# One tile per batch for the gated MLP's columns, and output weights read in two layouts

## The chip, the cores and the metric

The kernel runs on one core of one Trainium2 chip. The metric is device time of one execution in microseconds. All matrix work is in float32 or in pairs of rounded float32 parts ("high" and "low"), since the result is compared in float32.

## What is computed

Three layers follow one another: attention of 4,096 rows and 256 state rows to each other, a gated MLP, and a soft mixture of experts whose routing runs over all 4,608 rows.

```python
scores = scale * np.matmul(x, state.transpose(0, 1, 3, 2))
a = softmax(scores);           xread = np.matmul(a, state)
a2 = softmax(scale * np.matmul(state, x.transpose(0, 1, 3, 2)))
sread = np.matmul(a2, x)
x = concatenate([xread, sread])                # 4608 rows of 512
xn = x / sqrt(mean(x * x) + 1e-06) * rms_g
h = silu(xn @ w_gate) * (xn @ w_val)           # 512 -> 1536
x = h @ w_out                                  # 1536 -> 512
logits = x @ phi                               # 512 -> 32 slots
d = softmax(logits, over rows)
slot_input = d.T @ x                           # 8 experts x 4 slots
slot_out = relu(slot_input @ w1[e]) @ w2[e]    # 512 -> 1024 -> 512
out = softmax(logits, over slots) @ slot_out
```

The kernel never forms `h @ w_out` for all rows. It takes the logits from `h` through the folded matrix `wphi` = w_out phi, sums `E^T h` over the rows (E: exponentials of the logits) and multiplies by w_out once at the end.

## The kernel before

**Tiling.** The rows are eight batches of 512, g = 0 to 7, and a group of 256 with the state's rows (`sread`, group 8). The 1,536 MLP columns are three chunks c of 512, each of four tiles of 128. The work proceeds in units (g, c, t): one tile of 128 columns for 512 rows. A unit has a gate half and a value half (gv 0 and 1): `main_mm` issues six products 128x512 of `A` (normalised attention, high and low part) with the batch's weights `wp`; ScalarE makes `sg` = silu (L476), VectorE makes `hT` = value times `sg` (L485) and later turns it in 32x32 squares in place (`turn`, L492). Four products a chunk add to the logits (`lg_mm`). `sw` makes `wp` for one chunk and half (eight products on TensorE, a ScalarE copy L443, a VectorE step L444).

**A batch's end.** When its third chunk is done, `post1` to `post3` update the running maximum and make E. Then `slot_h` multiplies E with the batch's turned `hT`: for each chunk, each 32-row block and each of four squares of rows one product of 32x32 weights with 128 columns, into four PSUM banks (two from the pool `mm`, which the units use too, two from `misc`); four VectorE steps (L599) add them to `acc`. All products of float32 take two instructions.

**Order.** A stage is what runs while one batch's units run: stage 0 has batch 0 and the first chunk of batch 1 (16 units), stage 1 the other 8 of batch 1, each later stage 12. A table `at(unit, place, step)` fixes at which unit, and at which of two places in it, a step of the preparation for later batches is put; the queues then run in that order. The slot products of batch g stand at about the third unit of stage g+1. DMAs go out on SyncE's queue, in order.

**Weights.** They lie in memory as the bits of float64. `wload` fetches 1 MB, `wconv` makes float32 of it: two ScalarE operations (L179, L182), six of VectorE (two each of L195, L199, L203) and two adds on GpSimd (L207). The order is gate and value weights, then six loads of w_out. A converted w_out is stored as float32 (`w_out32`, six times 512 KB), read back for the end, and transposed on TensorE and multiplied with phi in `wphi_part` (six parts in stages 0 and 1). `conv1` at the table's units does the next conversion and load.

**Buffers.** `k8` holds 19 tiles of 8 KB a partition, for raw weights, `A`, `hT` and, later, the experts' weights, which `prefetch` asks for.

**The end.** After the sread group come the product with w_out, the experts in pairs, whose weights stream in, and the output.

```python
for c in range(NC):
    h = HT.pop((g, c))[:, : gsize(g), :]...
    for b in range(nb):
        o = 32 * (b % 4)
        for f in range(4):
            fs = slice(32 * f, 32 * f + 32)
            mm(pss[f][o : o + 32, c * P : (c + 1) * P], ET[fs, b, :], h[fs, :, b, :], ...)
```

## Time and profile before

| | before |
|---|---|
| median of 3 runs (lowest to highest) | 778.26 us (777.56 to 781.26) |
| the profiled execution | 776.07 us |
| its span | 774.0 us |
| TensorE (PE) busy | 666.7 us, 86% |
| weight loads (PEld) busy | 421.1 us, 54% |
| VectorE (DVE) busy | 464.0 us, 60% |
| ScalarE (ACT) busy | 335.1 us, 43% |
| GpSimd (POOL) busy | 107.5 us, 14% |
| read from HBM, written | 73.47 MB, 12.06 MB |

A busy share is a mean over the span. The chain of waits tells which engine sets the end; the rows below are from it, from the groups of instructions by cost, and from views of single stretches. PE is TensorE's products, PEld its weight loads, which overlap them. PEclk is the granted share of TensorE's full clock. The line numbers in the rows are those of the kernel before; nearly all products are recorded at the helper's line L85, transposes at L107, so the tiles tell them apart.

### The profile page before, as it was taken

To read this page: it belongs to the slowest core of one execution; us is meant where nothing else is said; L and a number is where in the kernel's file an instruction comes from. 1 tells how busy PE (TensorE), PEld (TensorE's weight loads), DVE (VectorE), ACT (ScalarE), POOL (GpSimd) and SP (SyncE) were. 2 spreads that over 40 slices of the span, in tenths; PEclk is the share of its full clock that TensorE was granted. 3 is DMA by queue.
4 is the path that set the end of the run, shared out by engine and by line. 5 is a ranking of instruction groups with operands and counts; after the bars stand their busy time and mean duration, and the time that the engine had idled before them with its cause. 6 is when DMAs were issued, how large, how long until landed. Compare 5 with 4: busy or idle time off the path is not lost.

```text
span 774.0 us, 17621 instructions
## 1 busy us (share of the span) xinstructions
PE 666.7 (86%) x7660; PEld 421.1 (54%) x7660; DVE 464.0 (60%) x942; ACT 335.1 (43%) x519; POOL 107.5 (14%) x129
## 2 busy tenths in 40 slices
PE   6496789997996999799799989989996996969990
PEld 4153456455554665455555656655654685944350
DVE  6848798875783477446546754675693475342251
ACT  6247473564382447236443833654321452200061
POOL 2304364220011011000101010110100000001340
PEclk9669898999999999999899999999997997988995
DMA  9920054511101011001101010100028033886948
GB/s 352 409 82 5 0 218 166 189 61 82 42 19 61 4 55 34 27 6 55 61 1 49 10 58 3 55 3 1 1 101 310 28 109 113 322 273 242 386 149 338
DMA packets 31972, 86.65 MB, mean 112 GB/s; under 512 B 1816, under 2 KB 3992, under 8 KB 29080
## 3 DMA queue, kind: packets, MB, share of 16 engines
q1 hardware_dynamic: 31608, 85.47, 30.2%
q8 instruction: 60, 0.98, 0.5%
q14 instruction: 16, 0.13, 0.1%
q10 hardware_dynamic: 288, 0.07, 0.0%
HBM read 73.47 MB, written 12.06 MB: 110 GB/s over the span
## 4 chain that ended last, share of the span: by engine, by line
PE 68%; DVE 18%; issue 7%; ACT 3%; DMA 1%; POOL 0%; DVEq 0%; ACTq 0%; POOLq 0%
PE mm L85 41%; PE misc L85 17%; PE lg L85 4%; PE misc L107 4%; DVE wp L444 2%; DVE hT L492 2%; DVE w L195 2%; PE so L85 2%; DVE w L203 2%; DVE hT L485 2%; DVE w L199 1%; ACT wp L443 1%; DMA raw_t<-in_w_gate_dram 1%; DVE wo L195 1%; DVE rinv L423 1%
## 5 line engine op out<-in xcount | busy, mean ns | idle before, releaser
L85 PE MATMUL mm<-A,wp 128*128 128x512 f32 x1152 | 302.9, 411 | 0.3 <-DVE hT L485 0.3
L85 PEld LDWEIGHTS mm<-A,wp 128*128 128x128 f32 x1152 | 216.0, 194 | 95.6 <-issue 44.1
L485 DVE TENSOR_TENSOR hT<-mm,sg 128x512 f32<-128x512 f32 x102 | 69.5, 683 | 73.9 <-PE mm L85 48.1
L476 ACT ACTIVATE sg<-mm 128x512 f32<-128x512 f32 x102 | 61.1, 599 | 97.3 <-PE mm L85 84.5
L85 PE MATMUL misc<-w,stTg 64*32 64x512 f32 x768 | 77.9, 624 | 15.8 <-DVE wp L444 7.9
L492 DVE STREAM_TRANSPOSE hT<-hT 128x512 f32<-128x512 f32 x102 | 69.6, 694 | 22.6 <-PE lg L85 22.6
L85 PE MATMUL mm<-hT,E 32*32 32x128 f32 x1632 | 54.0, 307 | 30.8 <-issue 26.1
L443 ACT CAST wp<-misc 128x512 fp32r<-128x512 f32 x96 | 51.5, 589 | 48.0 <-PE misc L85 47.6
L476 ACT ACT_TABLE_LOAD x27 | 34.6, 1283 | 78.6 <-PE mm L85 78.2
L444 DVE TENSOR_TENSOR wp<-misc,wp 128x512 fp32r<-128x512 f32 x96 | 61.6, 674 | 6.1 <-ACT wp L443 5.3
L85 PE MATMUL misc<-hT,E 32*32 32x128 f32 x1632 | 53.9, 308 | 12.4 <-issue 11.4
L85 PEld LDWEIGHTS mm<-hT,E 32*32 32x32 f32 x1632 | 38.5, 109 | 39.8 <-issue 30.5
L85 PEld LDWEIGHTS misc<-w,stTg 64*32 64x32 f32 x768 | 14.7, 107 | 61.5 <-issue 25.7
L85 PEld LDWEIGHTS misc<-hT,E 32*32 32x32 f32 x1632 | 37.6, 109 | 15.1 <-issue 12.8
L599 DVE SCALAR_TENSOR_TENSOR acc<-acc,al,mm 128x384 f32<-128x384 f32 x16 | 9.1, 610 | 52.3 <-PE misc L85 52.3
L85 PE MATMUL lg<-hT,wphi 128*32 128x512 f32 (+1 forms) x216 | 38.4, 580 | 0.3 <-DVE hT L485 0.3
L85 PE MATMUL mm<-xsg,wh 128*128 128x256 f32 x192 | 36.0, 289 | 0.0
L207 POOL TENSOR_TENSOR w<-w,raw 128x512 int32<-128x512 int32 x20 | 29.5, 1485 | 39.7 <-ACT wp L443 16.1
L302 POOL TENSOR_TENSOR a<-a,asum 128x1024 f32<-128x1024 f32 x7 | 13.6, 1947 | 142.9 <-PE mm L85 65.8
L415 POOL TENSOR_TENSOR rinv<-ra,rs_magic 128x128 int32<-128x128 int32 x10 | 4.1, 413 | 207.7 <-DVE ra L411 207.7
L85 PEld LDWEIGHTS mm<-xsg,wh 128*128 128x128 f32 x192 | 30.6, 196 | 2.5 <-issue 1.6
L396 ACT CAST A<-aT 128x1024 fp32r<-128x1024 f32 x8 | 8.4, 1046 | 46.7 <-DVE aT L392 37.0
(187 smaller groups left out, 895.5 us busy)
## 6 DMA issues: line engine op xcount, KB each, us to landing
ew<-in_w_dram SPq DMA_DIRECT2D x27, 1024.0 KB, 7.7
xT<-in_x_t_dram SPq DMA_DIRECT2D x8, 1024.0 KB, 5.0
xn<-in_x_n_dram SPq DMA_DIRECT2D x8, 1024.0 KB, 4.9
raw<-in_w_val_dram SPq DMA_DIRECT2D x6, 1024.0 KB, 17.0
out_dram<-ob SPq DMA_DIRECT2D x6, 1024.0 KB, 12.0
ew_w<-in_w_dram SPq DMA_DIRECT2D x5, 1024.0 KB, 9.8
raw<-in_w_gate_dram SPq DMA_DIRECT2D x4, 1024.0 KB, 14.2
raw_t<-in_w_out_dram SPq DMA_DIRECT2D x3, 1024.0 KB, 5.8
```

Of the source, the lines that this page charges most:

```text
L85: nc.tensor.matmul(out=o, lhsT=lhsT, rhs=rhs, start=start, stop=stop)
L107: nc.tensor.transpose(o, i, ident)
L195: nc.vector.tensor_scalar(out=dst[:, h], in0=dst[:, h], scalar1=EXP_LO, scalar2=EXP_HI, op0=ALU.max, op1=ALU.min,)
L203: nc.vector.scalar_tensor_tensor(out=a[:, h], in0=hi[:, h], scalar=-0x40000000, in1=a[:, h], op0=ALU.bitwise_and, op1=ALU.bitwise_or,)
L207: nc.gpsimd.tensor_tensor(out=a[:, h], in0=a[:, h], in1=rnd[:, h], op=ALU.add)
L302: (eng or nc.gpsimd).tensor_tensor(out=a3, in0=a3, in1=asum.unsqueeze(2).to_broadcast([P, 32, 32]), op=ALU.mult)
L443: nc.scalar.copy(t[:, r, 0, :], ps)
L444: nc.vector.tensor_tensor(out=t[:, r, 1, :], in0=ps, in1=t[:, r, 0, :].bitcast(F32), op=ALU.subtract)
L476: nc.scalar.activation(out=sg, in_=ps, func=AF.Silu)
L485: nc.vector.tensor_tensor(out=HT[g, c][:, q // (2 if g == sread_group else 1), :], in0=ps, in1=sg, op=ALU.mult)
L492: nc.vector.transpose(out=h, in_=h)
L599: nc.vector.scalar_tensor_tensor(out=o, in0=o, scalar=Q[g, "al"], in1=i, op0=ALU.mult, op1=ALU.add)
```

## The change

1. `hT` of a batch is one tile of 24 KB a partition (`k24`, two buffers, paid for by six of the 19 `k8` buffers), and `slot_h` takes all twelve column tiles in one product: 64 products of 384 columns a batch in place of 192 of 128. The sread group, which keeps two tiles, has products of 256 and of 128 columns.
2. w_out is also given to the kernel transposed, as float64 bits like the others (`w_out_t`, six more loads of 1 MB). `wphi_part` multiplies the converted transposed tile with phi directly: the transposes on TensorE and the copies on ScalarE go. The six loads and conversions of w_out itself, now for `w_out32` alone, go one to each of the stages 1 to 6.
3. The low part of `A` is made on GpSimd for all batches, before for batches 2 to 7 only.
4. At the start one conversion stands behind the first batch's normalisation (`att_ss`, `att_A`) in place of ahead of it.
5. In the stages, `sw` of the two halves of a chunk stands in two units following one another, before at one place.
6. Some raw weights and expert weights lie in thirds of `k24` tiles (`IN_HT`, `more_slices`), and the last stage asks for three loads at its unit 4 where it asked for two at unit 0 and two at unit 8.

The diff's core:

```diff
-        return big.tile([P, 4, 512], dt, tag="k8", bufs=19, name=f"{name}_{cnt[name]}")
+        return big.tile([P, 4, 512], dt, tag="k8", bufs=13, name=f"{name}_{cnt[name]}")
+    def k24(name, dt=F32):
+        return big.tile([P, 12, 512], dt, tag="k24", bufs=2, name=name)
...
-    order += [(3, c) for c in range(NC)]
+    order += [(gv, c) for gv in (2, 3) for c in range(NC)]
...
-        (nc.gpsimd if b > 1 else nc.vector).tensor_tensor(
+        nc.gpsimd.tensor_tensor(
             out=A[:, :, 1, :], in0=aT, in1=A[:, :, 0, :].bitcast(F32), op=ALU.subtract
...
-        for c in range(NC):
-            h = HT.pop((g, c))[:, : gsize(g), :].rearrange("p a b -> p (a b)").rearrange(
-                "p (q b j) -> p q b j", q=4, j=32
-            )
+        if g == sread_group:
+            parts = [(0, 8, HT.pop((g, 0))), (8, 4, HT.pop((g, 1))[:, :2, :])]
+        else:
+            parts = [(0, NF, HT.pop(g))]
+        for q0, q, h in parts:
+            h = h.rearrange("p a b -> p (a b)").rearrange("p (q b j) -> p q b j", q=q, j=32)
             for b in range(nb):
...
-                        pss[f][o : o + 32, c * P : (c + 1) * P], ET[fs, b, :], h[fs, :, b, :],
+                        pss[f][o : o + 32, 32 * q0 : 32 * (q0 + q)], ET[fs, b, :], h[fs, :, b, :],
...
     def wphi_part(c, j):
-        wo = WO.pop((c, j))
-        wt = k4("woT", [4, 2 * P])
-        for i in range(2):
-            ps = misc()
-            for d2 in range(2):
-                for k in range(2):
-                    o = (2 * d2 + k) * P
-                    q = 2 * i + d2
-                    transpose(ps[:, o : o + P], wo[:, k, q * P : (q + 1) * P])
-            nc.scalar.copy(wt[:, 2 * i : 2 * i + 2, :].rearrange("p a f -> p (a f)"), ps)
+        wt = WOT.pop((c, j))
+        ps = misc()
+        for k in range(2):
+            mm(ps[32 * k : 32 * k + 32, :], phis[:, 2 * j + k, :], wt[:, k, :])
+        if j == 0:
+            WPP[c] = k2("wpp")
+            nc.vector.tensor_copy(WPP[c][:64], ps[:64])
+            return
+        wp = WPP.pop(c)
+        nc.vector.tensor_tensor(out=wp[:64], in0=ps[:64], in1=wp[:64], op=ALU.add)
         ps = misc()
         for q in range(4):
-            mm(ps[32 * q : 32 * q + 32, : 2 * P], phis[:, q, :], wt[:, q, :])
-        wp = k2("wpp")
-        nc.vector.tensor_copy(wp[:, : 2 * P], ps[:, : 2 * P])
-        ps = misc()
-        for k in range(2):
-            mm(ps[:, 32 * k : 32 * k + 32], wp[:, k * P : (k + 1) * P], r32)
+            mm(ps[:, 32 * q : 32 * q + 32], wp[:64, q * P : (q + 1) * P], r32[:64])
...
-        conv1()
         att_ss(0)
         att_A(0)
+        conv1()
         sw(0, 0, 1)
...
                     at(4 * i - o, 2, sw, nb, c, 0)
-                    at(4 * i - o, 2, sw, nb, c, 1)
+                    at(4 * i - o + 1, 2, sw, nb, c, 1)
+            if g < 7:
+                at(4 if g == 1 else 1, 1, wload, 1)
+                at(6 if g == 1 else 2, 2, wconv, 1)
...
-                at(0, 2, prefetch, 2)
-                at(8, 1, prefetch, 2)
+                at(4, 2, more_slices)
+                at(4, 2, prefetch, 3)
```

Three places show how the instructions move. The first is TensorE at the end of batch 2's slot products, in stage 3; `mm<-A` are main products, `misc<-w,stTg` is `sw`, `lg` the logits. Before, 96 rows of slot products stand here, the last two of which are shown:

```order
L85 MATMUL mm<-hT_2578,E 32x128 x2
L85 MATMUL misc<-hT_2578,E 32x128 x2
L85 MATMUL mm<-A_2568,wp_2599 128x512 x6
L85 MATMUL mm<-A_2568,wp_2731 128x512 x6
L85 MATMUL mm<-A_2568,wp_2746 128x512 x6
L85 MATMUL lg<-hT_2725,wphi 32x512 x4
L85 MATMUL misc<-w_700,stTg 32x512 x8
L85 MATMUL misc<-w_780,stTg 32x512 x8
L107 MATMUL misc<-ident,sT 128x128 x4
```

And now, where 32 rows of slot products end:

```order
L88 MATMUL mm<-hT,E 32x384 x2
L88 MATMUL misc<-hT,E 32x384 x2
L88 MATMUL mm<-A_2225,wp_2294 128x512 x6
L88 MATMUL mm<-A_2225,wp_2387 128x512 x6
L88 MATMUL mm<-A_2225,wp_2452 128x512 x6
L88 MATMUL lg<-hT,wphi 32x512 x4
L88 MATMUL misc<-w_695,stTg 32x512 x8
L110 MATMUL misc<-ident,sT 128x128 x4
```

The products have three times the columns and stand before the same main products; the second `sw` has left this unit.

The second place is VectorE in the same stretch; `E` is the exponentials' turn, `c_all` and `cs` belong to the softmax over slots. Before:

```order
L566 STREAM_TRANSPOSE E<-E 128x512
L301 RECIPROCAL asum<-asum 128x32
L570 TENSOR_REDUCE cmax<-c_all 128x4
L571 TENSOR_TENSOR c_all<-c_all,cmax 128x128
L485 TENSOR_TENSOR hT_2725<-mm,sg 128x512
L611 TENSOR_REDUCE cs<-c_all 128x4
L612 TENSOR_SCALAR cs<-cs 128x4
L615 RECIPROCAL cs<-cs 128x4
L616 TENSOR_TENSOR c_all<-c_all,cs 128x128
L599 SCALAR_TENSOR_TENSOR acc<-acc,al,mm 128x12x32 x2
L599 SCALAR_TENSOR_TENSOR acc<-acc,al,misc 128x12x32 x2
L485 TENSOR_TENSOR hT_2725<-mm,sg 128x512
```

And now:

```order
L589 TENSOR_REDUCE cmax<-c_all 128x4
L497 TENSOR_TENSOR hT<-mm,sg 128x512
L590 TENSOR_TENSOR c_all<-c_all,cmax 128x128
L206 TENSOR_SCALAR wo_2500<-wo_2500 128x512 x2
L210 TENSOR_SCALAR wo_2500<-wo_2500 128x512 x2
L214 SCALAR_TENSOR_TENSOR wo_2500<-raw_2415,wo_2500 128x512 x2
L632 TENSOR_REDUCE cs<-c_all 128x4
L633 TENSOR_SCALAR cs<-cs 128x4
L636 RECIPROCAL cs<-cs 128x4
L637 TENSOR_TENSOR c_all<-c_all,cs 128x128
L620 SCALAR_TENSOR_TENSOR acc<-acc,al,mm 128x12x32 x2
L620 SCALAR_TENSOR_TENSOR acc<-acc,al,misc 128x12x32 x2
```

The six operations of a w_out conversion have come between the maximum over slots (`cmax`) and the steps of `acc`.

The third is VectorE at the start; L408 begins the chain that makes `rinv`, the rows' norms, and L435 ends it. Before, with more operations of the same conversion ahead:

```order
L195 TENSOR_SCALAR w_218<-w_218 128x512
L199 TENSOR_SCALAR w_218<-w_218 128x512
L203 SCALAR_TENSOR_TENSOR w_218<-raw_104,w_218 128x512
L408 TENSOR_SCALAR rv<-misc 128x128
L411 TENSOR_SCALAR ra<-rv 128x128
```

And now:

```order
L432 SCALAR_TENSOR_TENSOR ra<-ra,rv 128x128
L435 SCALAR_TENSOR_TENSOR rinv<-ra,rinv 128x128
L404 TENSOR_TENSOR aT<-aT,misc 128x1024
L206 TENSOR_SCALAR w_216<-w_216 128x512
L210 TENSOR_SCALAR w_216<-w_216 128x512
L214 SCALAR_TENSOR_TENSOR w_216<-hT,w_216 128x512
```

The conversion follows the end of the chain and `aT`, where it stood ahead of the chain's start; A's low part has left VectorE.

## Rows read from the trace of the kernel before

**Rows 1.** Page, part 4: the chain, share of the span by engine.
```profile
PE 68%; DVE 18%; issue 7%; ACT 3%; DMA 1%; POOL 0%; DVEq 0%; ACTq 0%; POOLq 0%
```

**Rows 2.** Page, part 5: group | busy us, mean ns | idle before it us, releaser.
```profile
L85 PE MATMUL mm<-hT,E 32*32 32x128 f32 x1632 | 54.0, 307 | 30.8 <-issue 26.1
...
L85 PE MATMUL misc<-hT,E 32*32 32x128 f32 x1632 | 53.9, 308 | 12.4 <-issue 11.4
```

**Rows 3.** Windows, nine slots: length, PE, PEld, DVE, ACT, POOL busy, PEclk, DMA, GB/s.
```profile
584.30:596.54 12.24, 8.02 (x385) 6.36 (x385) 0.78 (x4) 0.00 (x0) 0.00 (x0) 0.64 0.87 316
644.40:657.10 12.70, 7.41 (x384) 5.90 (x384) 4.31 (x10) 2.88 (x6) 0.00 (x0) 0.68 0.29 97
685.10:692.00 6.90, 3.21 (x192) 2.52 (x192) 0.56 (x3) 0.00 (x0) 0.00 (x0) 0.84 0.98 348
sum 92.29, PE 53.76 PEld 43.51 DVE 19.25 ACT 17.21 POOL 11.69; mean PE 5.97 PEld 4.83 DVE 2.14 ACT 1.91 POOL 1.30
```

**Rows 4.** Chain of waits, batch 2's slot stretch: start us, length us, what.
```profile
306.94 1.15 issue
...
309.99 3.48 issue
...
313.91 5.91 PE mm L85 x18
```

**Rows 5.** Windows view, batch 2's slot products ahead of the first gap.
```profile
303.40:306.94 3.54, 3.54 (x246) 3.08 (x246) 3.40 (x7) 2.19 (x3) 2.32 (x2) 1.00 0.02 7
```

**Rows 6.** Page, parts 1 (busy, instructions) and 3 (queue: packets, MB, share).
```profile
PE 666.7 (86%) x7660; PEld 421.1 (54%) x7660; DVE 464.0 (60%) x942; ACT 335.1 (43%) x519; POOL 107.5 (14%) x129
...
q8 instruction: 60, 0.98, 0.5%
```

**Rows 7.** Windows view, 18 main products behind the slots of batches 1, 3, 4.
```profile
243.85:249.25 5.40, 5.40 (x23) 4.09 (x26) 2.82 (x5) 1.27 (x1) 0.00 (x0) 0.79 0.00 0
385.23:391.54 6.31, 6.31 (x23) 4.79 (x26) 2.87 (x5) 1.28 (x1) 0.00 (x0) 0.66 0.00 0
454.14:458.45 4.31, 4.31 (x23) 3.30 (x26) 2.78 (x5) 1.27 (x1) 0.00 (x0) 1.00 0.02 4
```

**Rows 8.** Timeline of TensorE, a logits group: start us, length us, what.
```profile
319.74 1.06 PE L85 MATMUL lg<-hT,wphi 128*32 128x512 f32 x8
```

**Rows 9.** Timeline of TensorE, one part of wphi.
```profile
122.98 1.16 PE L107 MATMUL misc<-ident,wo 128*128 128x128 f32 x8
...
130.90 0.64 PE L85 MATMUL misc<-woT,phis 128*32 128x256 f32 x8
132.08 0.63 PE L85 MATMUL misc<-r,wpp 128*128 128x32 f32 x4 [0.54 <-DVE wpp L639]
```

**Rows 10.** Timeline of VectorE, then of TensorE, at the start.
```profile
28.70 0.42 DVE L195 TENSOR_SCALAR w<-w 128x512 f32<-128x512 f32 x1
...
33.67 0.28 DVE L408 TENSOR_SCALAR rv<-misc 128x128 f32<-128x128 f32 x1
...
38.93 2.05 PE L85 MATMUL misc<-rinv,ident 128*128 128x128 f32 x8 [8.92 <-DVE rinv L423]
```

**Rows 11.** Page, part 5: making of the per-batch weights on TensorE.
```profile
L85 PE MATMUL misc<-w,stTg 64*32 64x512 f32 x768 | 77.9, 624 | 15.8 <-DVE wp L444 7.9
```

**Rows 12.** Timeline of VectorE, behind batch 2's slot products.
```profile
313.93 1.14 DVE L599 SCALAR_TENSOR_TENSOR acc<-acc,al,mm 128x384 f32<-128x384 f32 x2 [6.80 <-PE misc L85]
```

**Rows 13.** Timeline of VectorE, one conversion of w_out.
```profile
132.02 2.41 DVE L195 TENSOR_SCALAR wo<-wo 128x512 f32<-128x512 f32 x2
...
134.48 0.75 DVE L199 TENSOR_SCALAR wo<-wo 128x512 int32<-128x512 int32 x2
135.15 1.28 DVE L203 SCALAR_TENSOR_TENSOR wo<-raw,wo 128x512 int32<-128x512 int32 x2
```

**Rows 14.** Page, part 6: DMA issues, count, KB each, median us to landing.
```profile
ew<-in_w_dram SPq DMA_DIRECT2D x27, 1024.0 KB, 7.7
...
raw<-in_w_val_dram SPq DMA_DIRECT2D x6, 1024.0 KB, 17.0
```

More of the change, by code (lines that the diff above doesn't have):

```diff
@@ L133 @@
     w_out32 = dram.tile([DFF, DM], F32, name="w_out32")
-    bits = {0: w_gate.bitcast(I32), 1: w_val.bitcast(I32), 3: w_out.bitcast(I32)}
+    bits = {
+        0: w_gate.bitcast(I32), 1: w_val.bitcast(I32), 2: w_out_t.bitcast(I32),
+        3: w_out.bitcast(I32),
+    }
     order = [(0, 0), (1, 0), (0, 1), (1, 1), (0, 2), (1, 2)]
-    order += [(3, c) for c in range(NC)]
+    order += [(gv, c) for gv in (2, 3) for c in range(NC)]
     to_load = [(gv, c, j) for gv, c in order for j in range(2)]
@@ L139 @@
     to_conv = list(to_load)
-    RAW, W, WO = {}, {}, {}
+    RAW, W, WOT = {}, {}, {}
     def wload(n):
@@ L146, in wload @@
             gv, c, j = to_load.pop()
-            n_raw = 18 - len(to_load)
-            if n_raw in IN_TMP:
+            n_raw = 24 - len(to_load)
+            if n_raw in IN_HT:
+                i = IN_HT[n_raw]
+                t = HT[1][:, 4 * i : 4 * i + 4, :].bitcast(I32)
+            elif n_raw in IN_TMP:
                 t = tmp.tile([P, 4, 512], I32, tag="raw", name=f"raw_t{n_raw}")
@@ L163 @@
     begun = []
+    IN_HT = {2: 0, 3: 1, 4: 2, 11: 1, 12: 2}
+    HT = {1: k24("hT")}
     IN_TMP = (1, 9, 13, 15, 17)
@@ L209, in wconv @@
                 )
+            if gv == 2:
+                WOT[c, j] = d2
             if gv == 3:
-                WO[c, j] = d2
                 r0 = c * 512 + 2 * j * P
@@ L447, in sw @@
         WP[b, c, gv] = t
-    HT, LGP = {}, {}
+    LGP = {}
     xsg_t = {}
@@ L479, in main_h, with hT_rows, hT_chunk @@
     def main_h(g, c, q, ps, sg):
-        if q == 0:
-            if g == sread_group and c == 1:
-                HT[g, 1] = HT[g, 0][:, 2:, :]
-            else:
-                HT[g, c] = k8("hT")
-        nc.vector.tensor_tensor(
-            out=HT[g, c][:, q // (2 if g == sread_group else 1), :], in0=ps, in1=sg, op=ALU.mult
-        )
+        if g == sread_group:
+            if q == 0 and c != 1:
+                HT[g, c // 2] = k8("hT")
+        elif g not in HT:
+            HT[g] = k24("hT")
+        nc.vector.tensor_tensor(out=hT_rows(g, c, q), in0=ps, in1=sg, op=ALU.mult)
+    def hT_rows(g, c, q):
+        return hT_chunk(g, c)[:, q // 2 if g == sread_group else q, :]
+    def hT_chunk(g, c):
+        if g == sread_group:
+            return HT[g, c // 2][:, 2 * (c % 2) : 2 * (c % 2) + 2, :]
+        return HT[g][:, 4 * c : 4 * c + 4, :]
     def turn(g, c, q):
-        h = HT[g, c][:, q, :]
+        h = hT_rows(g, c, q)
         nc.vector.transpose(out=h, in_=h)
@@ L498, in lg_mm @@
         lg = LGP[(g,)]
-        hT = HT[g, c][:, :n, :].rearrange("p a b -> p (a b)").rearrange("p (q t) -> p q t", q=4)
+        hT = hT_chunk(g, c).rearrange("p a b -> p (a b)").rearrange("p (q t) -> p q t", q=4)
         for q in range(4):
@@ L675, in sread_prep, with more_slices @@
         xsg_t["xsg"] = xsg
-    WH = {}
+    WH, slices = {}, []
+    def more_slices():
+        x = k24("x")
+        slices.extend(x[:, 4 * i : 4 * i + 4, :] for i in range(3))
     def w_split(gv, c):
@@ L710, in prefetch @@
                 return
-            k = loads.pop()
-            if home is None:
+            k, at_home = loads.pop(), home
+            if home is None and slices:
+                t = at_home = slices.pop(0)
+            elif home is None:
                 t = k8("ew")
+            elif home not in exp_pool:
+                t = home
             else:
@@ L722, in prefetch @@
             nc.sync.dma_start(out=t, in_=src)
-            EW[k], ew_home[k] = t, home
+            EW[k], ew_home[k] = t, at_home
     def take(k):
@@ L735, in conv1 @@
         wconv(n)
-        if to_load and (to_load[-1][0] < 2 or len(RAW) < 3):
+        if len(to_load) > 6 and (to_load[-1][0] < 2 or len(RAW) < 3):
             wload(n)
@@ L967 @@
                     lg_mm(*now)
-                    for q in range(gsize(now[0])):
-                        at(u + q // 2, 2 - q // 2, turn, *now, q)
+                    for q in range(0, 4, 2 if now[0] == gs else 1):
+                        at(u + q // 3, 2 - q // 3, turn, *now, q)
                     if now[1] == NC - 1:
@@ L976 @@
                         at(u + 2, 1, slot_h, pg)
+                        if pg == gs - 1:
+                            at(u + 2, 1, more_slices)
             if u == len(halves) - 1 and t == 0:
@@ L993 @@
     keep_warm(6)
-    for q in range(gsize(gs)):
+    for q in (0, 2):
         turn(gs, NC - 1, q)
```

10 lines of the change are left out of this document (4 added, 6 removed).

## The prediction, made before the changed kernel ran

> **What bounds the kernel now.** I read the chain of waits first. It runs through TensorE for 68% of the span, and 7% of it is "issue", time in which an engine waited for nothing that the profile shows [rows 1]. So the question is what TensorE does, and where it stands still for no visible reason. The list of costliest groups answers the second part: the products of `slot_h`, the ones that read `hT` and `E`, carry 26.1 and 11.4 us of idle time released by "issue", 37.5 us together [rows 2]. That is most of the chain's 7%, 54 us of 774.
>
> Next I cut the span into the nine stretches from the first slot product to the next main product. They last 92.29 us, in which TensorE is busy 53.76 us [rows 3]. The chain inside batch 2's stretch shows where the rest is: two gaps, 1.15 and 3.48 us, with nothing else waited for, and after them 18 main products that take 5.91 us [rows 4]. After batch 4's stretch the same 18 take 4.31 us at a granted clock of 1.00; after batch 3's they take 6.31 us at 0.66, after batch 1's 5.40 us at 0.79 [rows 7]. So a long gap is paid twice: TensorE stands still, and then the next products run partly at the lower of its two clocks, 1.2 instead of 2.4 GHz.
>
> What is the gap? Ahead of the first gap of batch 2 lie 246 products and 246 weight loads in 3.54 us [rows 5]; 136 ns for two, where the main products take 4.31 us for 18, 240 ns for one [rows 7]. The queue that carries instructions moved 0.98 MB in 60 packets, and TensorE has 7,660 products and 7,660 loads, so a packet holds about 256 of them [rows 6]. I read the gaps as TensorE using up its code faster than it is brought. A slot stretch has 384 products and 384 loads, three packets' worth, in under 6 us of work.
>
> **The change part by part.** The forecast is summed against the profiled execution, 776.07 us (span 774.0 and 2.1 us around it).
>
> *Slot products.* 192 products of 128 columns per batch (two instructions each) become 64 of 384. Instructions go from 768 to 256 a batch, columns stay. What is left of the time? The logits give the price of a column in this type: 8 instructions on 4 column strips, so two rounds of 512 columns, take 1.06 us [rows 8], 133 ns for 128 columns. A slot batch runs on 16 squares of 32x32, so 24 rounds; active time is 5.85 us a batch, from the 53.76 us less the two slow batches and the short one, 35.1 / 6 [rows 3], hence 244 ns a round, of which 111 ns are not columns. After the change there are 8 rounds of 398 + 111 ns: 4.1 us. Bounds: 3.2 us if the 111 ns vanish, 5.85 us if nothing shrinks. I take 4.1, because the columns are measured and the loads stay one per round.
> The two slow batches, 8.02 and 7.41 us of busy time at a clock of 0.64 and 0.68 [rows 3], shrink by the same 4.1 / 5.85, to 5.6 and 5.2; the short group has 4 rounds of 256 and 4 of 128 columns, with the same 111 ns: 2.5 us. New total 6 x 4.1 + 5.6 + 5.2 + 2.5 = 37.9 against 92.3: **-54.4 us**, of which 37.5 are the gaps. With 256 products and loads in 4.1 us a packet lasts as long as two did before, so I forecast no gap.
>
> The Trainium skill (Runtime: NRT & Kernel Launch, section on instruction fetch mechanics) says that code comes in 16 KiB blocks of 256 instructions and that crossing a block is mostly hidden. The block agrees with the 0.98 MB in 60 packets [rows 6]; "mostly hidden" does not agree with 37.5 us of gaps [rows 2]. By that rule the gaps would be something else and would stay; this is rival 3.
>
> *Main products behind a gap.* Batches 1, 2 and 3 lose 1.1, 1.6 and 2.0 us there against batch 4 [rows 4, 7]; without gaps the clock has no reason to fall: **-4.7 us** (0 if it falls anyway).
>
> *`wphi`.* Per part, 16 transposes, 8 products and 4 small ones take 1.16 + 0.64 + 0.63 us of TensorE, with 0.54 us of waiting [rows 9]; six parts: 14.6 us. Now a part is two products of 512 columns on two strips, two rounds, 1.06 us by the logits row; and every second part has eight small instructions, twice 0.63. Sum 6.4 + 3.8 = 10.2: **-4.4 us** (bounds 0 and -4.4; the waiting stays). ScalarE's copies go too; they were not on the path.
>
> *The start.* The conversion that stood ahead of the normalisation on VectorE, from 28.70 to 33.67 us, goes behind it; TensorE waited 8.92 us for that chain [rows 10]. At best everything after moves up 5 us; but the second half of the value weights is then converted later, and the first unit wants it. I take **-2 us** (0 to -5).
>
> *Weights per batch.* The two makings of a chunk's weights go to neighbouring units. TensorE waited 7.9 us in all for VectorE between them [rows 11]; I take **-5** (0 to -7.9).
>
> *The six moved conversions.* One w_out conversion per stage 1 to 6 now stands on VectorE right behind the slot's exponent, ahead of the four `acc` steps and the next `hT`. One costs VectorE 0.75 + 0.75 + 1.3 us undisturbed, and 2.41 for the first two instead of 0.75 where another engine disturbs it: 2.8 to 4.5 us [rows 13]. Before, VectorE idled 6.80 us in this place, waiting for TensorE's slot products [rows 12]. That cover shrinks to about 4 us. After the slot TensorE has two half units (2 x 6 x 0.24 = 2.9 us) before it wants the banks that `acc` frees, and a third before the logits want the next `hT`. VectorE: conversion 4.5 from the slot's start, row sums about 1, `acc` 2 x 1.14 [rows 12], `hT` 0.7: 8.5 us; TensorE: 4.1 + 4.3 = 8.4. So the wait is near zero when all is well and 2 us when disturbed; I take 1 us, **+6 us** (0 to +21, where the 3.5 us of a stretched conversion show whole).
>
> *Small ones.* A's low half goes from VectorE to GpSimd for batches 0 and 1, and batch 0's is on the path; the nearest row, a pair of VectorE operations on as many elements beside a busy GpSimd, took 2.41 us [rows 13]: **+1** (0 to +2.4). The expert loads are asked for about one load later; a load takes 7.7 us to land and eight of them feed the end [rows 14]; most have slack: **+2** (0 to +6). The added 6 MB of transposed weights lie in the first 120 us, where TensorE waits for conversions whose number is unchanged there: 0.
>
> Sum: -54.4 - 4.7 - 4.4 - 2 - 5 + 6 + 1 + 2 = **-61.5**, so 714.6 us for an execution like the profiled one. The median of the runs, 778.26, lies 2.2 us above that one, which makes **717 us**.
>
> **The rivals.**
> 1. *Half of the gaps stay.* There is still about one block of code in every slot stretch, and if a later one comes only 1.2 to 3.5 us after it is wanted, as in batch 2 [rows 4], half of 37.5 us stays, with its slow products: 717 + 19 + 2 = 738 us. For it: the 3.48 us gap is as long as the 246 pairs ahead of it took. Against: a block now lasts 4.1 us; 256 of the old pairs' instructions lasted half as long. Chance 0.13.
> 2. *The active time does not shrink*, because the price is by columns and not by rounds. Then 53.8 us stay in place of 37.9: 16 us more, 733 us. For it: columns are the same number. Against: only 133 of 244 ns are columns. Chance 0.13.
> 3. *The gaps are not code.* Something in a slot stretch then holds TensorE whatever the number of its instructions, and all gaps stay: 717 + 37.5 + 4.7 = 759 us. No row speaks for it, and the packets speak against it [rows 6]. The rule cited from the Trainium skill (Runtime: NRT & Kernel Launch, instruction fetch mechanics) would have it so. Chance 0.04.
> 4. *The conversions show in full*: 717 + 15 to 20 = about 735 us. For it: `acc` and `hT` stand behind them in VectorE's order. Chance 0.10.
> 5. *Slower than before.* VectorE works in order. If the raw load of a stage's conversion lands late, VectorE stands in front of `acc` and `hT`, and TensorE runs dry after two half units. The load is issued about a unit ahead of the stage and used in its fourth unit, at least 4 x 12 x 0.24 = 11.5 us later; such loads took 17.0 us to land at the crowded start [rows 14]. To eat 61 us, six stages must lose over 10 us each, so landing must take over 21 us. Against it: the DMA share is 0.02 in the first part of such a stretch [rows 5]. Chance 0.03.
> The main case keeps 0.57.
>
> **How the numbers follow.** The main case's own terms, at their ends, run from 717 - 6 x 0.9 (slot) - 3 (start) - 2.9 (weights) - 6 (conversions) = 700 to 717 + 15 (conversions) + 4.7 (clock) = 737. Cases 1, 2 and 4 lie at 733 to 738; the range 700 to 742 takes them in with some spread and leaves out cases 3 and 5 and the outer tails. A measurement tells about 0.5%, 3.9 us, from no change. All but case 5 are faster by more: faster 0.95, same 0.02, slower 0.03.
>
> **What would show it.** The slot rows should be 32x384, 1,152 product instructions with the short group's in place of 3,264, with idle time by "issue" near zero; a slot stretch of some 4 us; 18 main products behind it in 4.3 us; the instruction queue with some 43 packets; the wait of `acc` for TensorE's slot products gone from VectorE. A chain that passes from the conversion to `acc` to TensorE would show case 4; "issue" left in the slot stretch, cases 1 or 3. The forecast is wrong if the slot stretch stays above 6 us, or if TensorE waits for VectorE more than 2 us behind it.

## The result, and the profile after

The changed kernel takes 731.39 us (median of 4 runs, 730.83 to 736.45); the kernel before, run beside it, 778.47 us. The ratio is 0.9398, with a 95% interval of 0.9355 to 0.9442: faster by 6%, 47 us. The forecast was 717 us, in a range of 700 to 742; the direction is right, the range holds the time, and the middle lies 14 us too low. The profiled execution, 736.45 us, is the longest of the four. Totals below are therefore told by ratios or medians, and places by the trace.

The page of the changed kernel, parts 1, 3 and 4:

```profile
PE 651.6 (89%) x5476; PEld 381.7 (52%) x5476; DVE 491.6 (67%) x973; ACT 346.4 (47%) x523; POOL 128.8 (18%) x143
...
q8 instruction: 43, 0.70, 0.4%
...
PE 57%; DVE 18%; DMA 4%; ACT 3%; issue 3%; POOL 1%; SPq 0%; ACTq 0%; DVEq 0%; POOLq 0%
```

TensorE has 2,184 products and as many loads fewer than before [rows 6]; the instruction queue moved 43 packets instead of 60, and "issue" on the chain fell from 7% to 3% [rows 1]. Part 5 of the page, the groups that answer to [rows 2], and the main products:

```profile
L88 PE MATMUL mm<-A,wp 128*128 128x512 f32 x1152 | 303.0, 408 | 16.8 <-DVE acc L620 7.0
...
L88 PE MATMUL mm<-hT,E 32*32 32x384 f32 (+2 forms) x576 | 32.0, 473 | 3.9 <-DVE E L585 3.0
...
L88 PE MATMUL misc<-hT,E 32*32 32x384 f32 (+2 forms) x576 | 31.8, 474 | 0.7 <-ACT sq L383 0.7
```

The 37.5 us released by "issue" are gone from the slot products. In their place the main products wait 7.0 us for VectorE's `acc`, a wait that the kernel before did not show. The windows view of the nine slot stretches, with the columns of [rows 3]:

```profile
190.56:195.55 4.99, 4.32 (x128) 2.11 (x128) 2.85 (x8) 3.53 (x6) 0.00 (x0) 1.00 0.01 3
...
299.43:303.05 3.62, 3.62 (x128) 2.33 (x128) 3.62 (x8) 3.60 (x5) 1.92 (x1) 1.00 0.02 5
...
616.29:619.83 3.54, 3.54 (x129) 2.01 (x129) 0.12 (x1) 3.53 (x6) 0.00 (x0) 1.00 1.05 396
647.71:650.03 2.32, 2.32 (x128) 1.74 (x128) 0.56 (x4) 0.00 (x0) 0.00 (x0) 1.00 1.05 407
sum 32.47, PE 31.79 PEld 19.30 DVE 21.61 ACT 25.57 POOL 9.60; mean PE 3.53 PEld 2.14 DVE 2.40 ACT 2.84 POOL 1.07
```

The stretches take 32.5 us in place of 92.3, TensorE is busy through nearly all of it, and its clock is granted in full in every one. That is 5 us better than the forecast's 37.9. So the loss against the forecast lies elsewhere. From the first slot product of one batch to that of the next, in the two profiled executions (us):

| from, to | before | after | difference |
|---|---|---|---|
| start, batch 0 | 182.9 | 190.6 | +7.7 |
| 0, 1 | 49.0 | 44.8 | -4.2 |
| 1, 2 | 71.6 | 64.1 | -7.5 |
| 2, 3 | 70.6 | 64.5 | -6.1 |
| 3, 4 | 71.6 | 64.5 | -7.1 |
| 4, 5 | 67.0 | 64.5 | -2.5 |
| 5, 6 (stage 6) | 71.7 | 74.5 | +2.8 |
| 6, 7 | 60.0 | 48.9 | -11.1 |
| 7, short group | 40.8 | 31.4 | -9.4 |
| short group, end | 88.9 | 86.7 | -2.2 |

Two rows have the wrong sign: the time up to the first slot product, and stage 6. Both scatter between traces: with the same start the first slot product stands at 184.8 to 190.6 us in the kernels below, and stage 6 takes 72.2 us in two of them (e1, e10) whose edits do not touch it. VectorE and TensorE behind batch 2's slot products, in the timeline (start, length, what, idle before it), show the new wait:

```profile
300.27 1.58 DVE L590 TENSOR_TENSOR c_all<-c_all,cmax 128x128 f32<-128x128 f32 x1
301.77 0.75 DVE L206 TENSOR_SCALAR wo<-wo 128x512 f32<-128x512 f32 x2
302.44 0.75 DVE L210 TENSOR_SCALAR wo<-wo 128x512 int32<-128x512 int32 x2
303.11 1.28 DVE L214 SCALAR_TENSOR_TENSOR wo<-raw,wo 128x512 int32<-128x512 int32 x2
304.32 0.27 DVE L632 TENSOR_REDUCE cs<-c_all 128x4 f32<-128x128 f32 x1
304.62 0.97 DVE L633 TENSOR_SCALAR cs<-cs 128x4 f32<-128x4 f32 x1
...
305.84 1.12 DVE L637 TENSOR_TENSOR c_all<-c_all,cs 128x128 f32<-128x128 f32 x1
306.88 1.12 DVE L620 SCALAR_TENSOR_TENSOR acc<-acc,al,mm 128x384 f32<-128x384 f32 x2
```

```profile
303.05 3.04 PE L88 MATMUL mm<-A,wp 128*128 128x512 f32 x12
307.54 1.66 PE L88 MATMUL mm<-A,wp 128*128 128x512 f32 x6 [1.45 <-DVE acc L620]
```

VectorE runs without a gap from 300.27; TensorE does its two half units and stands 1.45 us for the bank that `acc` frees. The conversion takes 2.8 us. Two of the small operations behind it take 0.97 us (`cs`, L633) and 1.12 us (`c_all` by `cs`, L637); before, the same two took 0.17 and 0.29 us. In their time GpSimd is at work on the conversion's own two additions (from 304.11, 2.70 us). The 1.58 us of `c_all` less its maximum, beside an addition of the attention on GpSimd (299.78 to 301.70), are not new: before, this operation took 2.05 us in this place, under the cover of the slot products.

### The profile page after: what moved, and what is told of

It reads as the page before. It is cut to its first block, busy times and chain, and to the rows that moved or that the text cites. A ratio compares the mean times of both kernels' runs of the same rounds, so it can differ in the third digit from the quotient of the medians.

```text
span 734.4 us, 13336 instructions
## 1 busy us (share of the span) xinstructions
PE 651.6 (89%) x5476; PEld 381.7 (52%) x5476; DVE 491.6 (67%) x973; ACT 346.4 (47%) x523; POOL 128.8 (18%) x143
## 4 chain that ended last, share of the span: by engine, by line
PE 57%; DVE 18%; DMA 4%; ACT 3%; issue 3%; POOL 1%; SPq 0%; ACTq 0%; DVEq 0%; POOLq 0%
PE mm L88 34%; PE misc L88 16%; PE lg L88 4%; DVE wp L456 3%; DMA x<-in_w_dram 2%; PE misc L110 2%; DVE wo L214 2%; DVE wo L206 2%; DVE hT L497 1%; ACT wp L455 1%; DMA out_dram<-ob 1%; DVE c_all L590 1%; DVE wo L210 1%; DVE hT L511 1%; DVE c_all L637 1%
## 5 line engine op out<-in xcount | busy, mean ns | idle before, releaser
L88 PEld LDWEIGHTS mm<-A,wp 128*128 128x128 f32 x1152 | 211.0, 191 | 127.7 <-issue 47.3
L88 PE MATMUL misc<-w,stTg 64*32 64x512 f32 x768 | 74.4, 645 | 8.4 <-POOL w L218 4.8
L88 PE MATMUL lg<-hT,wphi 128*32 128x512 f32 (+1 forms) x216 | 40.7, 597 | 0.3 <-DVE hT L497 0.3
L88 PE MATMUL mm<-hT,E 32*32 32x384 f32 (+2 forms) x576 | 32.0, 473 | 3.9 <-DVE E L585 3.0
L88 PEld LDWEIGHTS misc<-w,stTg 64*32 64x32 f32 x768 | 11.4, 107 | 44.9 <-issue 21.2
L88 PE MATMUL misc<-hT,E 32*32 32x384 f32 (+2 forms) x576 | 31.8, 474 | 0.7 <-ACT sq L383 0.7
L409 POOL TENSOR_TENSOR A<-aT,A 128x1024 fp32r<-128x1024 f32 x8 | 20.3, 2532 | 59.3 <-ACT A L408 59.3
L218 POOL TENSOR_TENSOR wo<-wo,raw 128x512 int32<-128x512 int32 x18 | 24.5, 1375 | 27.1 <-DVE wo L214 20.0
L408 ACT CAST A<-aT 128x1024 fp32r<-128x1024 f32 x8 | 8.4, 1047 | 42.3 <-DVE aT L404 42.3
L383 ACT ACTIVATE sq<-misc 128x512 f32<-128x512 f32 x32 | 17.5, 595 | 21.3 <-PE misc L88 21.3
L88 PE MATMUL mm<-xsg,wl 128*128 128x256 f32 x96 | 27.1, 283 | 0.0
```

The costliest lines, as they stand in the source:

```text
L88: nc.tensor.matmul(out=o, lhsT=lhsT, rhs=rhs, start=start, stop=stop)
L218: nc.gpsimd.tensor_tensor(out=a[:, h], in0=a[:, h], in1=rnd[:, h], op=ALU.add)
L383: nc.scalar.activation(out=sq[:, m, :], in_=pss[m], func=AF.Square)
L409: nc.gpsimd.tensor_tensor(out=A[:, :, 1, :], in0=aT, in1=A[:, :, 0, :].bitcast(F32), op=ALU.subtract)
```

## The experiments

Twelve more kernels ran, each beside runs of the kernel before. All are edits of the changed kernel, whose ratio is 0.9398.

**The start.** The conversion back where it was:

```diff
+        conv1()
         att_ss(0)
         att_A(0)
-        conv1()
         sw(0, 0, 1)
```

> The changed kernel with one edit undone: the start's second conversion of value weights stands ahead of the first batch's normalisation again. Theory (the reordering lost time: unit 1's main products began 5.1 us later than before, because the conversion met A's low half on GpSimd and held back the weights of the value half): 4 to 6 us faster than the changed kernel, about 726 us, unit 1 beginning near 51.5 us instead of 56.5. Rival (stage 0 is held by the sum of VectorE's conversions whatever their order): within 1.5 us of the changed kernel, the later start caught up by unit 12.

723.61 us, ratio 0.9319 (0.9274 to 0.9364): 6 us faster than the changed kernel by the ratios, 7.8 by the medians. The first slot product stands at 180.8 us in place of 190.6. Traces of other kernels here with the changed start have it at 184.8 to 190.6, so part of the 9.8 us is scatter of the start; 180.8 to 182.0 is what the four kernels with this edit show. The changed kernel's timeline at the start, of VectorE, GpSimd and TensorE, shows what happens there:

```profile
41.47 2.57 DVE L206 TENSOR_SCALAR w<-w 128x512 f32<-128x512 f32 x1
```

```profile
41.18 2.58 POOL L409 TENSOR_TENSOR A<-aT,A 128x1024 fp32r<-128x1024 f32 x1 [7.61 <-ACT A L408]
43.72 1.47 POOL L218 TENSOR_TENSOR w<-w,hT 128x512 int32<-128x512 int32 x1
```

```profile
36.65 2.04 PE L88 MATMUL misc<-rinv,ident 128*128 128x128 f32 x8 [4.18 <-DVE rinv L435]
...
43.81 1.22 PE L88 MATMUL mm<-A,wp 128*128 128x512 f32 x2 [1.44 <-POOL A L409]
45.24 1.91 PE L88 MATMUL misc<-w,stTg 64*32 64x512 f32 x2 [0.21 <-POOL w L218]
```

The normalisation did come earlier, but only by 2.3 us (36.65 against 38.93 in [rows 10]). The conversion, now behind it, meets A's low half on GpSimd: a VectorE operation of 0.42 us takes 2.57, as long as GpSimd's own, and the additions that finish the value weights queue behind GpSimd's 2.58 us. The value half of unit 0 comes behind them. That this stretching is the reason is not shown; A's low half is tested by itself below.

**The moved conversions.** Away from the slot, at unit 7 of stages 2 to 6:

```diff
-                at(6 if g == 1 else 2, 2, wconv, 1)
+                at(6 if g == 1 else 7, 2, wconv, 1)
```

> The changed kernel with the w_out conversions of stages 2 to 6 at unit 7 instead of unit 2, away from the slot products. Theory (the conversion delays acc, and TensorE waits 1.3 to 1.45 us for it, five times, 7.0 us in all): the wait of the main products for acc falls to under 1.5 us in all, 5 to 8 us faster than the changed kernel, about 725 us. Rival (VectorE's work has to go somewhere and shows as another wait at unit 7 or 8): within 2 us of the changed kernel, with a new wait of TensorE for wp, hT or the normalisation of about 1.4 us a stage.

723.39 us, ratio 0.9309 (0.9264 to 0.9353): 7 us faster by the ratios, 8 by the medians. The four steps from batch 1 to batch 5 take 62.5 to 62.7 us instead of 64.1 to 64.5, and the 18 main products behind the slot stand in one row:

```profile
295.74 4.38 PE L88 MATMUL mm<-A,wp 128*128 128x512 f32 x18
...
326.84 1.13 PE L88 MATMUL misc<-rinv,ident 128*128 128x128 f32 x8 [0.92 <-DVE rinv L435]
```

The wait for `acc` is gone; the second row is the price at the new place, 0.92 us in this stage, where the conversion comes between the steps of the normalisation. So TensorE's idle time falls by only 0.3 us from batch 2's slot products to batch 3's; its busy time falls by 1.5 us (61.13 to 59.65). There the logits' products, which want the next `hT`, had taken 4.8 us and take 3.2: `hT` too was late. Conversions behind the slot cost 7 to 8 us net.

**The columns of a slot product.** Cut again, into three of 128 columns, or two of 192 (W = 6):

```diff
+        W = 4
         for q0, q, h in parts:
+            for q1 in range(0, q, W):
+                n = min(W, q - q1)
...
-                        pss[f][o : o + 32, 32 * q0 : 32 * (q0 + q)], ET[fs, b, :], h[fs, :, b, :],
+                            pss[f][o : o + 32, 32 * (q0 + q1) : 32 * (q0 + q1 + n)],
+                            ET[fs, b, :], h[fs, q1 : q1 + n, b, :],
```

> The changed kernel with each slot product of 384 columns cut into three of 128, as before the change: 768 instructions of TensorE a batch instead of 256, the same columns, nothing else changed. Theory (code comes too slowly, and each round of products has a fixed cost): gaps by issue of 25 to 40 us in all in the slot products, active time 5.8 instead of 3.5 us a batch, clock lower behind the gaps: 45 to 65 us slower than the changed kernel, 776 to 796 us. Rival (most of the gain came from the other edits): under 25 us slower.

772.68 us, ratio 0.9928 (0.9896 to 0.9960): 41 us slower than the changed kernel, nearly the time before. It lies just under the range that was expected.

> The changed kernel with each slot product of 384 columns cut into two of 192: 512 instructions a batch. Theory of rounds: 16 rounds of 200 + 111 ns, 5.0 us active, 1.5 us more a batch, 12 us in all; theory of code: two blocks of 256 instructions in 5 us, a gap of 0.5 to 2 us in most batches, 4 to 12 us in all. Both together: 14 to 25 us slower than the changed kernel, 745 to 756 us. If the gaps were tied to a stretch and not to the number of its instructions, none or all of the 37.5 us would be there: 12 or 50 us slower.

746.77 us, ratio 0.9588 (0.9522 to 0.9654): 15 us slower. The slot groups of the two, first 128 and then 192 columns, in the view of groups by line:

```profile
L88 PE MATMUL mm<-hT,E 32*32 32x128 f32 x1632 | 50.0, 284 | 11.9 <-issue 7.9 <-DVE E L585 3.1 <-DVE cs L636 0.9
L88 PE MATMUL misc<-hT,E 32*32 32x128 f32 x1632 | 49.6, 285 | 22.2 <-issue 21.3 <-ACT sq L383 0.9
```

```profile
L88 PE MATMUL mm<-hT,E 32*32 32x192 f32 (+2 forms) x1120 | 41.5, 330 | 5.5 <-DVE E L585 3.1 <-issue 1.5 <-DVE cs L636 0.9
L88 PE MATMUL misc<-hT,E 32*32 32x192 f32 (+2 forms) x1120 | 41.1, 331 | 11.3 <-issue 10.3 <-ACT sq L383 0.9
```

Gaps by issue: 29.2 us with 768 instructions a batch, 11.8 with 512, none in these groups with 256. The page of each shows 59, 51 and 43 packets of instructions. In the timeline nearly every batch has two gaps with 768 (1.0 to 3.2 us each) and one with 512; with 512 it is 0.73 to 0.95 us in batches 0 to 5, none in batch 6, but 2.31 us in batch 7 and 4.55 in the short group (384 instructions), where the expert loads keep the DMA engines busy (a share of 0.58 and 0.90 in these two stretches, 0.01 to 0.03 in the others). The places of the gaps tell what they are. In each of the 15 batches of the kernel before and of the 128-column kernel that have two gaps, the second comes exactly 128 products, with their loads 256 instructions, behind the first. With 192 columns the gap stands at the same product of its batch as the first one with 128 (the 165th in batch 5). So the gaps are code that comes too late. That it comes later where other transfers run is only my reading: in the kernel before, at shares of 0.30 to 0.36, gaps last from 1.03 to 4.03 us.
The active time of a batch, without gaps, is 5.76 us with 128 columns (batch 5: a stretch of 8.69 us less 1.38 and 1.55), 4.74 with 192 (5.69 less 0.95) and 3.6 with 384: 240, 296 and 450 ns a round. The line through the ends has 0.82 ns a column and 135 ns a round; it gives 292 ns for 192.

**The parts set apart.** Still 128 columns, but with a half unit of main products between the three chunks of a batch:

```diff
-                at(u + 3, 1, slot_h, pg)
+                at(u + 3, 1, slot_third, pg, 0)
+                at(u + 3, 2, slot_third, pg, 1)
+                at(u + 4, 1, slot_h, pg)
```

> As the kernel with products of 128 columns (e3_cols128, 772.7 us), but batches 0 to 6 do the slot products in three parts of 256 instructions, with a half unit of main products (six, about 1.4 us) between them; batch 7 and the short group stay whole. Theory (code comes at a limited rate, and the gaps are TensorE having used up what was fetched): between the parts more code arrives, so the idle time by issue in the slot products of batches 1 to 6 falls from 3.3 us a batch to under 1.5, in all from 29 to under 16 us; time about 757 to 766 us. Rival (a gap belongs to every block of 256 slot instructions, or to the PSUM banks they write): issue stays at 25 us or more, time 770 us or above.

763.50 us, ratio 0.9807 (0.9766 to 0.9848), 9 us faster than in one piece. The gaps:

```profile
L88 PE MATMUL misc<-hT,E 32*32 32x128 f32 x1632 | 53.3, 289 | 9.4 <-issue 8.4 <-ACT sq L383 0.9
L88 PE MATMUL mm<-hT,E 32*32 32x128 f32 x1632 | 53.2, 288 | 4.2 <-DVE E L585 3.1 <-DVE cs L661 0.9 <-issue 0.2
```

Of 8.6 us left, 8.4 lie in batch 7 and the short group, which had stayed whole; batches 0 to 6, cut apart, have 0.17 us together. The same instructions, spread, have next to no gaps: it is the rate at which they are used up, not their kind or the banks they write. The time falls by 9 us, less than the 20.6 us of gaps that are gone: from batch 0's slot products to batch 1's this kernel takes 55.4 us where the one in one piece takes 50.2, and the rest was not taken apart.

**Both repairs.** The edits of e1 and e2 together:

> The changed kernel with both edits: the start's conversion back ahead of the normalisation and the w_out conversions of stages 2 to 6 at unit 7. Theory (the two costs lie in different stages and add): 7 to 8 us from each, 714 to 718 us. Rival (each edit only shifted the same wait): 722 us.

716.37 us, ratio 0.9218 (0.9179 to 0.9257). The two costs add: by the ratios 6 and 7 us alone and 14 together, by the medians 8, 8 and 15. They lie in different stages.

**The weights per batch.** Both makings at one place:

```diff
-                    at(4 * i - o + 1, 2, sw, nb, c, 1)
+                    at(4 * i - o, 2, sw, nb, c, 1)
```

> The changed kernel with the two makings of a chunk's weights back at one place. Forecast's term: 5 us lost, mostly as TensorE's wait for VectorE's wp. Theory after reading the trace: in stages 2 to 5 about 1 us a stage is lost again, but in stage 6 the preparation of the short group no longer comes ahead of the second half's weights, where TensorE idled 3.35 us and then ran 10 us at half its clock, so some 5 to 8 us come back: within 4 us of the changed kernel. Rival (spreading was a plain gain): 5 to 8 us slower.

747.01 us, ratio 0.9602 (0.9566 to 0.9638): 16 us slower. Neither expectation holds. Stages 2 to 5 cost 0.2 to 0.4 us each (64.2 and 64.8 against 64.1 and 64.5). Stage 6 takes 71.7 us, 0.5 us less than in e1 and e10, the step after it loses 3.2. The bulk is in one place: from batch 0's slot products to batch 1's it takes 55.4 us instead of 44.8. This timeline of TensorE in stage 1 of that kernel shows how:

```profile
196.60 1.92 PE L88 MATMUL misc<-w,stTg 64*32 64x512 f32 x24
199.09 1.06 PE L88 MATMUL misc<-w,stTg 64*32 64x512 f32 x8 [0.57 <-DVE wp L456]
...
221.12 2.08 PE L88 MATMUL misc<-rinv,ident 128*128 128x128 f32 x8 [2.33 <-DVE rinv L435]
...
228.05 2.36 PE L88 MATMUL mm<-A,wp 128*128 128x512 f32 x9 [1.01 <-POOL A L409]
```

and in the changed kernel, in the same stage:

```profile
198.12 1.09 PE L88 MATMUL misc<-w,stTg 64*32 64x512 f32 x16
...
212.55 1.13 PE L88 MATMUL misc<-rinv,ident 128*128 128x128 f32 x8 [0.53 <-DVE rinv L435]
```

Sixteen instructions of one making take 1.09 us; two makings together, with three `misc` banks for four tiles, take 1.92 + 0.57 + 1.06, 1.4 us more than two times 1.09. In the steady stages nearly all of it is given back. In stage 1, which has only 8 units, TensorE waits for the normalisation of the next batch (2.33 and 1.01 us), and it is busy 49.7 us between the two slot starts where it was 43.0: of the 10.6 us, 6.7 are longer work and not waiting, at a mean granted clock of 0.97 against 1.00. Why its work is longer was not taken apart. One thing speaks against a plain price of the place: the kernel before had both makings at one place too, with the same 1.92, 0.57 and 1.06 us in stage 1. Outside batch 0's slot stretch this step took it 39.0 us, the changed kernel 39.8, and this one 50.3. So the loss arises only beside the other parts of the change.

**The preparation of the short group.** In stage 6 of the changed kernel TensorE waits 3.35 us for weights behind `sread_prep`, and then runs at about half its clock:

```profile
549.50 2.55 PE L88 MATMUL mm<-A,wp 128*128 128x512 f32 x8 [3.35 <-ACT wp L455]
```

```profile
552.00:562.00 10.00, 10.00 (x27) 3.22 (x26) 3.94 (x12) 2.67 (x4) 0.00 (x0) 0.54 0.91 343
```

The mean granted clock of 0.54 over ten microseconds is nearly the lower level, 1.2 GHz. The edit:

```diff
-                at(8, 2, sread_prep)
+                at(10, 2, sread_prep)
```

> The changed kernel with the short group's preparation in stage 6 at unit 10 instead of unit 8, behind the spread weights of unit 9. Theory (it stood ahead of those weights on VectorE and ScalarE; stage 6 took 74.5 us where the others take 64.5): stage 6 5 to 9 us shorter, about 723 to 727 us. Rival (the preparation then comes too late for the short group or hits the end of the batch): within 2 us, or slower.

729.88 us, ratio 0.9381 (0.9345 to 0.9417): not to be told from the changed kernel. Stage 6 is 6.6 us shorter (67.9 us; 4.3 against the 72.2 of e1 and e10), but the next step is 3.7 us longer (52.6), and this is where it went, in the window of batch 6's slot products:

```profile
556.80:564.12 7.32, 6.36 (x129) 2.97 (x129) 2.93 (x8) 2.44 (x4) 0.00 (x0) 0.79 0.95 351
```

```profile
563.28 0.51 PE L88 MATMUL mm<-hT,E 32*32 32x384 f32 x2 [0.96 <-issue]
```

Ahead of it TensorE waited 1.37 us for weights, the slot products meet the expert loads (DMA share 0.95), the clock falls to 0.79 in the mean, and the stretch takes 7.3 us instead of 3.6. The second row is a gap by issue of 0.96 us inside a batch of 256 instructions. The kernel with all four edits has one of 0.73 us in the same batch (DMA share 1.04); the changed kernel has none in batch 7 and the short group at a share of 1.05.

**A's low half** of batches 0 and 1 back on VectorE:

```diff
-        nc.gpsimd.tensor_tensor(
+        (nc.gpsimd if b > 1 else nc.vector).tensor_tensor(
             out=A[:, :, 1, :], in0=aT, in1=A[:, :, 0, :].bitcast(F32), op=ALU.subtract
```

> The changed kernel with A's low half of batches 0 and 1 on VectorE again. Forecast's term: 1 us (0 to 2.4). Theory: at the start GpSimd's 2.58 us for it stretched a conversion on VectorE (2.57 us for an operation of 0.42) and delayed the conversion's own additions, so its return gives 2 to 5 us: 727 to 730 us. Rival (hidden behind the conversions): within 1 us of 731.4.

734.36 us, ratio 0.9442 (0.9397 to 0.9487): not to be told from the changed kernel, and if anything slower. The conversion on VectorE is no longer stretched there (0.42 us for the operation that took 2.57), and the first slot product still stands at 189.4 us. So GpSimd was not the cause by itself at the start; the conversion's place was.

**All four edits** (start, conversions, preparation, A's low half):

> The changed kernel with four edits: the start's conversion back ahead of the normalisation, the w_out conversions of stages 2 to 6 at unit 7, the short group's preparation at unit 10, A's low half of batches 0 and 1 back on VectorE. Theory: on top of e6_start_conv (716.4 us), whose stage 6 still took 71.7 us with a wait of 7.0 us for weights, the move of the preparation gives 2 to 6 us and A's low half 1 to 2 us: 708 to 713 us. Rival (the preparation's gain is given back at the batch's end, as before): 715 to 717 us.

715.99 us, ratio 0.9201 (0.9169 to 0.9233): the same as e6_start_conv. The rival holds: more than half of the preparation's gain is given back in the next step (67.1 and 51.5 us where e6 has 71.7 and 48.9).

**The second part undone.** No transposed w_out; `wphi_part`, the loads and the conversions as before the change, all else as changed:

```diff
-    order += [(gv, c) for gv in (2, 3) for c in range(NC)]
+    order += [(3, c) for c in range(NC)]
...
-            if g < 7:
-                at(4 if g == 1 else 1, 1, wload, 1)
-                at(6 if g == 1 else 2, 2, wconv, 1)
```

> The changed kernel with its second part undone: no transposed w_out; w_out is converted in stages 0 and 1 only, transposed on TensorE and copied by ScalarE as before; nothing is converted in stages 1 to 6. Forecast's terms: 4.4 us of TensorE lost again, 6 us of conversions behind the slots saved. Theory after reading the trace: stage 0 waits for conversions and not for TensorE, so the 4.4 us come back only in part (0 to 3 us slower there), while the stages gain 7 to 8 us as in e2_conv_unit7: 723 to 727 us. Rival (the second part is a gain as a whole): 732 us or more.

716.28 us, ratio 0.9199 (0.9171 to 0.9228): 15 us faster than the changed kernel, where 4 to 8 were expected. In stage 0 nothing is lost, as the theory had it: the windows view from 117 us to the first slot product, first of this kernel, then of the changed one (columns as in [rows 3]):

```profile
117.00:188.17 71.17, 66.07 (x453) 36.64 (x453) 60.86 (x114) 35.24 (x54) 20.29 (x16) 0.95 0.43 149
```

```profile
117.00:190.56 73.56, 63.18 (x388) 31.15 (x386) 61.87 (x114) 33.96 (x47) 21.58 (x16) 0.91 0.33 116
```

TensorE has 2.9 us less to do in the changed kernel and is not done sooner; it is idle 10.4 us there instead of 5.1. Its waits in that window are for ScalarE's `sg` (3.2 us), VectorE's `e2T` (2.8) and `wpp` (1.7) and GpSimd's last step of a conversion (1.7). That the conversions, whose number is the same, stand behind the first two is my reading. With the start repaired, the first slot product stands at 180.8 to 182.0 us with the transposed w_out and at 182.0 without: worth about 1 us at most. The stages gain more than the 8 us of e2: 2.0 us from batch 0 to 1, 2 to 2.5 in each of the four steps after it, 5.4 in stage 6 (3.1 against e1 and e10), 3.1 behind the short group. With the conversion at unit 7 stage 6 took 74.5 us (e2) and 71.7 us (e6), without it 69.1, so it costs something there too; the 3.1 us at the end are not explained.

**The same with the start repaired:**

> As e11_no_wout_t (716.3 us), and the start's conversion back ahead of the normalisation. Theory (the start's loss lies before the first slot product and is independent of the second part): first slot product near 181 us instead of 188, 708 to 711 us, faster than every kernel so far. Rival (without the transposed weights the conversions of stage 0 are ordered differently, and the start's gain is caught up by unit 12): 714 us or more.

709.55 us, ratio 0.9156 (0.9120 to 0.9192), the fastest here: the wide slot products and the spread weights, without the transposed w_out and without the reordered start. The first slot product stands at 182.0 us instead of 188.2.

## Why the prediction was right or wrong

*The slot products* were right and the bulk of the gain. The theory of the gaps held at nearly every point: none with 256 instructions a batch, one with 512, two with 768, next to none with 768 spread out; the exceptions are the two gaps with 256 beside expert loads (0.96 and 0.73 us). The term of -54.4 us is -59.8 in the trace. Of the 5.4 us, 3.7 lie in batches 6 and 7, which the forecast left at a low clock (5.6 and 5.2 us) and which took 3.54 each at 1.00. Most of the rest is the price of a column, 0.82 ns where the logits row gave 1.04, while 135 ns a round stand where 111 were taken. The logits' 1.06 us hold an end that is paid once: in a later trace (e12) their second round starts 0.45 us behind the first, 0.88 ns a column. Rivals 1, 2 and 3 fall. With them falls, for this kernel, the sentence of the Trainium skill (Runtime: NRT & Kernel Launch, instruction fetch mechanics) that crossing a block is mostly hidden: here it cost 29 to 38 us where a block was used up in about 2 us, and nothing in the changed kernel, where it lasted 3.6. The blocks of 256 agree: 43, 51, 59 and 60 packets for 10,952, 13,128, 15,176 and 15,320 products and loads.

*The clock behind the gaps* was right: 1.00 in all nine stretches and behind those of batches 1 to 4.

*The moved conversions* were right in kind and near in size: +6 forecast, 7 to 8 measured by moving five of them. The mechanism is the one described, VectorE late with `acc` and `hT`, TensorE short of a bank after two half units. The conversion itself was not stretched (2.8 us); it starts 2.3 us behind the slot's start and not with it, and the row sums take 2.6 us (304.32 to 306.96) where "about 1" stood. This is rival 4 in a weak form.

*`wphi`* failed: "-4.4 us (bounds 0 and -4.4)". The work left TensorE: its products were busy 16.7 us before (a part has 8 transposes and not 16; the 1.16 us were for all 8) and 12.9 after. But their waits grew from 1.4 to 3.4 us, and the time up to the first slot product fell by about 1 us at most. I had costed busy time of an engine as if it set the end, since TensorE is busy for 0.97 of that stretch in the kernel before. It was the bound of 0 that held. The second part as a whole, -4.4 + 6 = +2 in the forecast, is +15 by its undoing, the price that rival 4 gave the conversions; how it divides is open, and the wait for `acc` is only 7.0 us of it.

*The start* failed in sign: "-2 us (0 to -5)" is +3 to +7 by three pairs with and without it (6 us from 0.9398 to 0.9319, 3 from 0.9199 to 0.9156, 7 from 0.9309 to 0.9218). I had written down the cost, that the value weights come later and the first unit wants them, and then took the gain of the normalisation as the larger.

*The spread weights* were mis-sized: -5 forecast, -16 by undoing. The row of waits [rows 11] did not hold the price: most of it is in stage 1, and the kernel before did not pay it there. So the 16 us are what spreading is worth beside the other parts, not what it gained over the kernel before.

*Stage 6* was not in the forecast at all. It was taken to be like the others and is 8 to 10 us longer. That the spread weights come behind the short group's preparation explains the waiting there; moving the preparation only moved the loss.

*A's low half* and *the expert loads*, +1 and +2: too small to be told. The end behind the short group is 2.2 us shorter although its slot stretch is 4.6 us shorter; TensorE waits 0.7 us there for an expert load, and the rest is open.

With each term of the forecast put into the step where it lies (an estimate from the table and the stretches), the profiled execution (736.45 us against 714.6) misses 22 us: 13 up to the first slot product, 7 in stage 6 and 1 to 2 in each of the five steps between, less 6 in the two steps behind stage 6, where the slot products did better. The median lies 5 us lower and its forecast 2 us higher, so it misses 14; the start alone scatters by 6. So the time lies in the range by errors of both signs, and because the range reached up to 742 for rivals 1, 2 and 4: that it holds the time is in part luck. The single undoings don't add up to the whole. The conversions' wait is there only because the slot stretch became short: with the conversions in the same place the main products wait 7.0 us for `acc` with 256 instructions a batch, 0.8 with 512 and 1.6 with 768.

## What to carry to other kernels

Where an engine stands still with nothing to wait for, count its instructions against the packets of its code queue: here many short products, 256 instructions in about 2 us, cost gaps, and fewer, longer ones or other work between them removed them. When a stretch that covered another engine's work shrinks to a third, ask what was under that cover before anything is added there. Work taken off a busy engine need not be worth its busy time, and what an undoing costs in the changed kernel need not be what the change gained: a repair in one stage counts only if nothing else in that stage is as late.
